# A new order for the same operations: attention and a squared-ReLU network on one core

## The chip, the core and the metric

The kernel runs on one core of one Trainium2 chip. Such a core has five engines that run side by side, each working through its own queue of instructions in order: TensorE (PE, matrix products; its loads of weights are shown apart as PEld), VectorE (DVE), ScalarE (ACT), GpSimd (POOL) and SyncE (SP), which here only issues transfers. Engines wait for each other by semaphores. Transfers between the chip's memory and the core's SBUF run on 16 DMA engines. Products land in PSUM, 8 banks of 2 KB a partition.

The metric is the device time of one execution in microseconds (us). Single executions of this kernel agree within about 0.1%.

## The reference

Inputs are q, k and v of 8 batches, 8 heads, 576 tokens and 64 dimensions, 16 "beacon" tokens of keys and values for each batch and head, and two weight matrices, w_in (512 x 2048) and w_out (2048 x 512).

```python
k_all = np.concatenate([beacon_k, k], axis=2)
v_all = np.concatenate([beacon_v, v], axis=2)
scores = scale * np.matmul(q, k_all.transpose(0, 1, 3, 2))
causal = np.zeros((S, Nb + S), dtype=bool)
causal[:, Nb:] = np.triu(np.ones((S, S), dtype=bool), k=1)
scores = np.where(causal, -1000000000.0, scores)
a = np.exp(scores - scores.max(-1, keepdims=True))
a /= a.sum(-1, keepdims=True) + 1e-09
attn = np.matmul(a, v_all)
x = attn.transpose(0, 2, 1, 3).reshape(B * S, H * D)
h = x @ w_in
r = np.maximum(h, 0.0)
out = (r * r) @ w_out
```

So each of the 4608 tokens gets a causal attention (the beacons are seen by all), and the 512 values of a token then go through a network of 2048 hidden units.

## The kernel before

**The attention.** Work is done a batch and a pair of heads at a time: pair p = 4 x batch + pair, 0 to 31. q and k come from memory in blocks and are transposed, so that the 64 dimensions of a head lie on partitions. Batch 0 and batch 1 are transposed by matmuls: L488 (batch 0, a first part of 240 tokens on the whole array, with 120 rows from two head pairs at a time, and a second part of 336 tokens, tp0.1.*, on halves of the array's columns, 64 at a time), L490 (batch 1, on halves of the columns too), and L453 for the beacons on 32 rows. From batch 2 on DMA transposes do it. The scores (L650, names qk) use halves of the array's rows: the two heads of a pair lie on 64 rows each. ACT takes the exponential (L672 in batch 0, L748 later), POOL (L777) or DVE (L781) masks the diagonal, and the product with v (L803, av) uses the whole array, with a column of ones that gives the sum. DVE takes the reciprocal (L820) and normalizes (L822, norm) out of PSUM into xn. xn is transposed to xT by matmuls (L871, xtp, with a copy xte) or by DMA.

**The network** works on nine chunks of 512 tokens, each as soon as its tokens' attention is there. Chunks 0 to 2 multiply by w_in plainly (L1093, s1), take relu (L1107 on ACT, L1109 on DVE) and the square (L1117, L1119); chunk 0 also multiplies by w_out plainly (L1142, s2). Later ones use seven products of halves in place of eight, with sums of weights (L929, L914) and of activations (L963, L966, L1171, L1174) made by DVE and POOL; their products are L990 and L1206, the partial results are kept in `spare` (L373, L375), joined (L1028) and squared (L1054, L1056), and the outputs are summed by DVE (L1229) and stored.

**Loads.** The first blocks of q and k come through SP and ACT, the other loads are issued by POOL: q (L409), k and v (L418, their beacons L417), strided blocks of q and k of batches 0 and 1 (L473), the four quarters of w_in (L894) and of w_out (L903). v has two buffers, one for even and one for odd batches.

**What sets the order.** Every operation is recorded under a name, and one long string, SEQUENCE (lines 17 to 167), lists all 1737 names. `Order.run` goes through it and issues each operation to its engine; a letter behind @ chooses the engine (A is ACT, D is DVE, P is POOL). Each engine then runs its own instructions in this order. Buffers that are shared (two `strip` tiles of two PSUM banks for the scores, four `ps` banks for all else, three `held` areas) are handed out first come first served, as the string goes.

```python
for word in SEQUENCE.split():
    name, _, letter = word.partition("@")
    op = named.pop(name)
    e = self.LETTER[letter] if letter else op.engs[0]
```

60 dummy matmuls (L355, fill, 128x256 on a tile of ones) are names in the string too; they go to places at the start where the order's maker expected TensorE to be idle.

Of the kernel before, what the change touches and what calls it, by code (L numbers as in the profile page):

```python
# [29 lines left out]
norm1.0.0 exp1.1.0 exp0.1.0 qk1.1.2 av3.0.0 norm0.0.0 tp0.1.3q fill18 fillg18 qk2.0.0 fill47 fillg47 norm3.0.0  # L30
exp1.1.2 exp2.0.0 eq0.1.3@D tpg0.1.3q tp0.1.2k fill45 fillg45 xtp0.0.0 fill0 xtp0.0.1 ek0.1.2@D tpg0.1.2k fillg0
qk0.1.2 mask2.0.0@D xte0.0.1@A xte0.0.0@D win0 qk0.1.1 fill4 fillg4 av2.0.0 fill56 fill24 fillg56 fill14 fill30
fillg24 fillg30 fillg14 norm2.0.0 tp0.1.2q fill5 tp0.1.3k fillg5 xtp0.0.2 xtp0.0.3 eq0.1.2@D exp0.1.2 exp0.1.1 qk1.1.1
xte0.0.2@A qk2.1.0 exp1.1.1 xte0.0.3@D s1.0.5.0 s1.0.6.0 mask0.1.1@P ld1v2 win3 bkc1 ek0.1.3@D exp2.1.0 mask0.1.0@P
sld1k0.0 mask1.1.1@P ld1v1 ld2q4 ld2q0 zero2 sld1q0.0 sld1k0.2 wout0 sld1q0.2 wout1 ld1v0 ld2k0 wout2 ld2q5 ld1v4
wout3 ld1v3 ld2k2 ld2q1 ld2q7 ld2k3 tpg0.1.2q tpg0.1.3k qk2.1.1 exp2.1.1 s1.0.4.0 s1.0.9.0 qk2.1.2 qk3.1.0 mask2.1.1@D
relu0.4.0@D relu0.9.0@D s1.0.10.0 mask2.1.0@D mask1.1.0@D relu0.6.0@A relu0.10.0@A exp3.1.0 av0.1.0 norm0.1.0 s1.0.7.0
av1.1.0 exp2.1.2 relu0.5.0@A s1.0.11.0 relu0.7.0@D sq0.3.0@A relu0.11.0@D norm1.1.0 mask3.1.1@D qk3.1.1 qk3.1.2
s1.0.2.0 s1.0.1.0 exp3.1.1 mask3.1.0@D relu0.1.0@D xtp0.1.1 exp3.1.2 xte0.1.1@A relu0.2.0@A av2.1.0 s1.0.0.0 xtp0.1.0
av3.1.0 norm2.1.0 relu0.0.0@D xte0.1.0@A s1.0.3.0 relu0.3.0@A norm3.1.0 s1.0.14.0 xtp0.1.2 s1.0.13.0 xtp0.1.3  # L40
relu0.14.0@A xte0.1.2@A s1.0.12.0 s1.0.8.0 relu0.13.0@D relu0.12.0@D relu0.8.0@D xte0.1.3@A s1.0.6.1 relu0.6.1@A
s1.0.13.1 s1.0.2.1 tpb1 ekb1 relu0.2.1@D s1.0.0.1 relu0.0.1@A relu0.13.1@D s1.0.11.1 relu0.11.1@A s1.0.1.1 s1.0.15.0
relu0.15.0@A sq0.7.0@A relu0.1.1@D tp1.0.0q s1.0.10.1 relu0.10.1@D tp1.0.0k ek1.0.0 eq1.0.0@A tpg1.0.0q tp1.0.1q
tp1.0.1k eq1.0.1@D s1.0.12.1 qk4.2 sq0.1.0@D relu0.12.1@A ek1.0.1 tpg1.0.1q tpg1.0.0k tpg1.0.1k s1.0.4.1 s1.0.7.1
relu0.7.1@D sq0.2.0@D s1.0.5.1 s1.0.14.1 relu0.4.1@A exp4.2.0.0.0 mask4.0.0.0@D relu0.5.1@A sq0.0.0@D exp4.2.1.0.0
s1.0.15.1 s1.0.9.1 relu0.9.1@D s1.0.3.1 qk4.4 sq0.3.1@D relu0.3.1@A relu0.15.1@D sq0.0.1@A sq0.1.1@D exp4.4.1.0.0
s1.0.8.1 tp1.0.2k tp1.0.2q relu0.8.1@D relu0.14.1@D sq0.4.0@A sq0.2.1@D sq0.6.1@D sq0.5.0@D sq0.4.1@D exp4.4.0.0.0
mask4.0.2@P ek1.0.2 s2.0.2.0 s2.0.0.0 s2.0.2.1 eq1.0.2@A sq0.5.1@D tpg1.0.2q tpg1.0.2k qk5.7 exp5.7.-1.1.0
exp5.7.1.0.0 exp5.7.-1.0.0 s2.0.0.1 tp1.0.3k exp5.7.0.0.0 mask4.0.0.1@P ld2q3 mask6.0.0.0@P ld2k4 ld2q2 ld2q6
mask4.0.1.1@D wsum1 mask4.0.1.0@D s2.0.0.2 tp1.0.3q s2.0.2.2 sq0.7.1@D ek1.0.3 eq1.0.3@A asum1 mask5.0.2@D  # L50
mask5.0.1.1@D tpg1.0.3k sq0.6.0@A tpg1.0.3q qk7.13 exp7.13.-1.0.0 s2.0.2.3 ev0.2@D exp7.13.0.0.0 exp7.13.-1.1.0
exp7.13.1.0.0 s2.0.0.3 s2.0.3.0 ev0.0@A mask5.0.0.1@P mask7.0.0.1@D mask7.0.1.0@D mask7.0.1.1@D mask7.0.2@D ld2v0
mask5.0.1.0@P ld2k1 ld2v2 qk6.10 exp6.10.-1.1.0 exp6.10.1.0.0 exp6.10.0.0.0 exp6.10.-1.0.0 mask6.0.1.1@P mask6.0.0.1@P
s2.0.3.1 av4.0.0 s2.0.3.2 mask7.0.0.0@D mask5.0.0.0@D av5.0.0 mask6.0.2@P mask6.0.1.0@D norm5.0.0 av7.0.0 norm7.0.0
norm4.0.0 tr2q tr2k s2.0.3.3 av6.0.0 av4.0.1 ev0.3@A s2.0.1.0 norm4.0.1 norm6.0.0 av6.0.1 av7.0.1 norm6.0.1 av5.0.1
s2.0.1.1 norm7.0.1 norm5.0.1 xtp1.0.0 xtp1.0.2 xte1.0.2@D xte1.0.0@A s2.0.1.2 xtp1.0.3 xtp1.0.1 s2.0.1.3 xte1.0.1@A
xte1.0.3@D s1.1.13.0 relu1.13.0@A asum2 s1.1.4.0 wsum2 relu1.4.0@D s1.1.15.0 ev0.1@A relu1.15.0@A s1.1.6.0 relu1.6.0@D
qk8.2 exp8.2.1.0.0 exp8.2.0.0.0 s1.1.7.0 s1.1.2.0 s1.1.0.0 qk8.4 relu1.7.0@A relu1.2.0@A exp8.4.1.0.0 s1.1.1.0
s1.1.14.0 relu1.1.0@A relu1.14.0@A exp8.4.0.0.0 s1.1.5.0 relu1.0.0@D mask8.0.0.0@D wsum3 wsum4 relu1.5.0@D s1.1.11.0
s1.1.12.0 sq1.2.0@A warm sq1.0.0@D relu1.11.0@D sq1.3.0@D s1.1.3.0 relu1.12.0@A sq1.6.0@A mask8.0.1.0@D s1.1.10.0  # L60
s1.1.8.0 s1.1.9.0 relu1.10.0@A relu1.3.0@D qk9.7 relu1.9.0@A exp9.7.-1.0.0 mask8.0.2@D mask8.0.0.1@D sq1.7.0@D
sq1.1.0@D mask8.0.1.1@D sum1.1.1@D sq1.5.0@D ld3q4 ld2v3 ld3q2 ld2v1 ld3q5 ld2v4 ld3v2 ld3q1 ld3k4 ld3k3 ld3k0 ld3q0
ld3v3 ld3k2 ld3q6 ld3q7 ld3k1 st1 st0 av8.0.0 relu1.8.0@D sq1.4.0@A exp9.7.-1.1.0 s2.1.1.0 av8.0.1 norm8.0.0
sum1.3.1@D s2.1.1.1 sum1.1.0@D sum1.3.0@D sum1.2.1@D sum1.2.0@D s2.1.2.0 s2.1.5.0 s2.1.2.1 exp9.7.1.0.0 exp9.7.0.0.0
ev1.c1.None@A norm8.0.1 ev1.c11.None mask9.0.0.1@D ld3v0 ld3q3 ld3v4 mask9.0.1.0@P mask9.0.1.1@P mask9.0.0.0@D tr3k
s2.1.6.0 qk10.10 s2.1.6.1 exp10.10.-1.0.0 exp10.10.-1.1.0 exp10.10.0.0.0 exp10.10.1.0.0 xtp2.0.0 mask9.0.2@D av9.0.0
s2.1.5.1 xte2.0.0@A mask10.0.1.0@P sum1.4.1@D ev1.u2.None@D s2.1.7.0 av9.0.1 s2.1.7.1 ev1.u3.None@A norm9.0.0
norm9.0.1 mask10.0.2@P mask10.0.0.1@P ld4k4 sum1.4.0@D mask10.0.0.0@D tr3q ld4k0 ld4q7 ld4q6 ld4k2 mask11.0.0.0@D
mask10.0.1.1@D qk11.13 exp11.13.-1.0.0 exp11.13.-1.1.0 exp11.13.1.0.0 exp11.13.0.0.0 s2.1.4.0 av10.0.0 s2.1.4.1
xtp2.0.1 mask11.0.1.0@P mask11.0.1.1@P mask11.0.0.1@P ev1.c22.None norm10.0.0 mask11.0.2@D ev1.c21.None@D xte2.0.1@A  # L70
s2.1.3.0 av10.0.1 norm10.0.1 qk12.2 exp12.2.0.0.0 av11.0.0 xtp2.0.2 av11.0.1 norm11.0.0 xte2.0.2@A exp12.2.1.0.0
s2.1.3.1 norm11.0.1 xtp2.0.3 xte2.0.3@A ev1.c12.None qk12.5 exp12.5.-1.0.0 exp12.5.1.0.0 s1.2.3.0 relu2.3.0@D
exp12.5.-1.1.0 exp12.5.0.0.0 s1.2.2.0 s1.2.9.0 s1.2.10.0 relu2.2.0@D asum4 qk13.8 relu2.9.0@A exp13.8.-1.0.0
exp13.8.1.0.0 exp13.8.-1.1.0 s1.2.6.0 s1.2.8.0 s1.2.0.0 exp13.8.0.0.0 mask12.0.1.0@D relu2.10.0@D relu2.6.0@D s1.2.1.0
# [1280 lines left out]
```

## Time and profile before

| | |
|---|---|
| median of 3 runs | 322.87 us (322.85 to 323.05) |
| the profiled execution | 323.34 us |
| its span, first to last instruction | 321.6 us |
| mean granted clock of TensorE | 0.998 |
| DMA traffic | 39.61 MB, mean 123 GB/s |

The page of the profile gives for each engine its busy time, its share of the span and its number of instructions. The timeline lists runs of instructions of the same kind on one engine: start and length in us, engine, line, operation, what it writes and reads, how many; a bracket at the end says how long the engine had been idle before and what released it. The length of such a run ends with the modelled end of its last matmul, which overlaps the next run, so two runs are compared from start to start. The chain of waits follows the end of the program back to its start, and its rows are start, length, engine, tile and line. The windows give the busy time of every engine in a stretch of the span (from:to, length, then each engine in the order of the head line, the granted clock, the mean number of busy DMA engines' share as listed, and GB/s).

The work falls into these stretches: to 7.84 us, first loads and dummy matmuls; to 19.72, batch 0's transposes, scores and av up to the first product with w_in; to 42.88, the rest of batch 0, chunk 0 against w_in and the first transposes of batch 1; to 68.92, chunk 0 against w_out, the other transposes and the first attention of batch 1; to 256, the attention of the other batches between the chunks; to 318, the last chunks alone; then the last sum and store.

### The profile page before, as it was taken

How to read it: one execution, taken by the hardware profiler on the slowest of the kernel's cores; microseconds unless marked ns; L12 is line 12 of the kernel's file. 1: busy time of each engine (PE TensorE's matmuls, PEld its weight loads, DVE VectorE, ACT ScalarE, POOL GpSimd, SP SyncE). 2: the span in 40 equal slices, each digit the busy share in tenths (PEclk: the TensorE clock that was granted, in tenths of full speed). 3: DMA queues.
4: the chain of work that ended last, by engine and by line, in shares of the span. 5: the costliest groups of instructions: out<-in, count | busy, mean ns of one | idle time of the engine just before them, and what ended most of it. 6: DMA issues, size and time to landing. Idle time of an engine off the chain costs nothing.

```text
span 321.6 us, 9484 instructions
## 1 busy us (share of the span) xinstructions
PE 314.5 (98%) x3882; PEld 247.3 (77%) x3882; DVE 249.6 (78%) x526; ACT 217.1 (68%) x324; POOL 196.9 (61%) x316
## 2 busy tenths in 40 slices
PE   7999999999999999999999999999999999999995
PEld 5679755744887469889888878888888878888884
DVE  2977696759966699879987999798877987697852
ACT  2787589268678694679678896889696653763320
POOL 9675387398169737697794779625436060555651
PEclk9999999999999999999999999999999999999999
DMA  8999999999969999999989959993701230110042
GB/s 154 184 193 191 197 182 124 222 162 130 175 53 119 138 177 154 127 171 193 105 123 178 190 56 126 142 126 95 128 2 67 79 65 0 67 65 2 16 151 98
DMA packets 153189, 39.61 MB, mean 123 GB/s; under 512 B 140730, under 2 KB 148794, under 8 KB 153146
## 3 DMA queue, kind: packets, MB, share of 16 engines
q0 software_dynamic: 103744, 18.10, 72.8%
q1 hardware_dynamic: 48253, 20.29, 30.0%
q10 hardware_dynamic: 1149, 0.62, 0.9%
q8 instruction: 30, 0.49, 0.6%
q14 instruction: 13, 0.11, 0.1%
HBM read 37.22 MB, written 9.44 MB: 145 GB/s over the span
## 4 chain that ended last, share of the span: by engine, by line
PE 91%; DVE 5%; issue 1%; ACT 1%; DMA 1%; POOL 0%; DVEq 0%; ACTq 0%; POOLq 0%
PE ps L1206 28%; PE ps L990 21%; PE ps L1093 13%; PE ps L803 8%; PE strip L650 7%; PE ps L1142 4%; PE ps L355 3%; PE ps L650 2%; PE strip L1206 2%; DVE g L1028 2%; DVE xn L822 1%; PE ps L871 1%; PE ps L488 1%; PE ps L490 1%; DMA xT<-xn 1%
## 5 line engine op out<-in xcount | busy, mean ns | idle before, releaser
L1206 PEld LDWEIGHTS <-g 128*128 128x128 bf16 x768 | 72.7, 97 | 10.6 <-issue 1.2
L748 ACT ACTIVATE pt<-strip 128x1024 bf16<-128x1024 f32 x70 | 70.9, 1032 | 5.4 <-PE strip L650 5.4
L1206 PE MATMUL ps<-w_out,g 128*128 128x256 bf16 x480 | 61.0, 272 | 0.0
L1028 DVE CUSTOM_DVE_ANT_0 g<-ps,spare 128x512 bf16<-128x512 f32 x72 | 48.7, 686 | 15.7 <-PE ps L990 11.2
L777 POOL TENSOR_SCALAR_AFFINE_SELECT pt<-pt 128x256 bf16<-128x256 bf16 (+1 forms) x78 | 31.9, 429 | 45.1 <-ACT pt L748 41.6
L373 ACT COPY spare<-ps 128x512 f32<-128x512 f32 x54 | 31.6, 588 | 23.9 <-PE ps L990 17.0
L1093 PE MATMUL ps<-xT,w_in 128*128 128x512 bf16 (+2 forms) x256 | 45.2, 326 | 0.0
L990 PEld LDWEIGHTS <-w_in 128*128 128x128 bf16 x480 | 39.4, 96 | 7.0 <-issue 2.5
L409 POOL DMA_DIRECT2D qk_area<-in_q_dram x48 | 35.0, 733 | 13.2 <-DMA qT<-qk_area 6.8
L990 PE MATMUL ps<-xT,w_in 128*128 128x256 bf16 (+4 forms) x384 | 41.8, 247 | 0.7 <-DVE g L1056 0.7
L1174 POOL TENSOR_TENSOR g<-g 128x256 bf16<-128x256 bf16 x44 | 29.6, 708 | 18.4 <-DVE g L1171 12.6
L803 PE MATMUL ps<-vb,pt 128*128 128x65 bf16 (+1 forms) x960 | 38.2, 193 | 0.1
L803 PEld LDWEIGHTS <-pt 128*128 128x128 bf16 (+1 forms) x960 | 35.5, 97 | 3.3 <-issue 0.6
L1093 PEld LDWEIGHTS <-w_in 128*128 128x128 bf16 x256 | 23.6, 98 | 17.2 <-issue 2.0
L418 POOL DMA_DIRECT2D vb<-in_v_dram x40 | 34.0, 851 | 1.2 <-DMA qk_area<-in_q_dram 0.7
L822 DVE TENSOR_TENSOR xn<-ps,rcp 128x320 bf16<-128x320 f32 (+2 forms) x64 | 31.5, 492 | 2.2
L1054 ACT ACTIVATE g<-g 128x1024 bf16<-128x1024 bf16 x30 | 31.1, 1067 | 2.3 <-DVE g L1028 1.5
L990 PEld LDWEIGHTS <-qk_area 128*128 128x128 bf16 x320 | 27.5, 97 | 5.5 <-issue 1.7
L748 ACT ACTIVATE pt<-ps 128x512 bf16<-128x512 f32 x42 | 24.0, 601 | 8.1 <-PE ps L650 6.9
L1206 PE MATMUL ps<-w_sum,g 128*128 128x256 bf16 x224 | 28.9, 272 | 0.0
L650 PEld LDWEIGHTS <-kT 64*128 64x128 bf16 x618 | 20.0, 94 | 11.1 <-issue 8.8
L418 POOL DMA_DIRECT2D qk_area<-in_k_dram x30 | 25.4, 850 | 4.2 <-DMA kT<-qk_area 1.8
(87 smaller groups left out, 502.0 us busy)
## 6 DMA issues: line engine op xcount, KB each, us to landing
out_dram<-osb SPq DMA_DIRECT2D x16, 512.0 KB, 3.5
qk_area<-in_q_dram POOLq DMA_DIRECT2D x48, 72.0 KB, 4.9
vb<-in_v_dram POOLq DMA_DIRECT2D x24, 128.0 KB, 6.0
qk_area<-in_k_dram POOLq DMA_DIRECT2D x18, 128.0 KB, 4.5
w_in<-in_moe_w_in_dram POOLq DMA_DIRECT2D x4, 512.0 KB, 10.9
w_out<-in_moe_w_out_dram POOLq DMA_DIRECT2D x4, 512.0 KB, 10.6
vb<-in_v_dram POOLq DMA_DIRECT2D x8, 112.0 KB, 4.4
qk_area<-in_k_dram POOLq DMA_DIRECT2D x6, 112.0 KB, 4.7
```

The costliest lines, as they stand in the source:

```text
L373: nc.scalar.copy(dst, src)
L409: return [nc.gpsimd.dma_start(out=qb[:, g, :, D * u:D * u + D], in_=t[b, c].rearrange("(n p) d -> p n d", p=NP))]
L418: insts.append(nc.gpsimd.dma_start(out=dst[lo:rows], in_=t[b, :, t0:t0 + rows - lo, :].transpose([1, 0, 2])))
L650: nc.tensor.matmul(out, kc[b % 2][hp, c, pr] if b >= NPE else kT[b % 2][hp, pr, 128 * c:128 * c + 128], rhs, start=True, stop=True)
L748: nc.scalar.activation(out, in_, AF.Exp, bias=0.0, scale=scale)
L777: nc.gpsimd.affine_select(out=d[:, :, i], in_=d[:, :, i], compare_op=ALU.is_ge, fill=0.0, base=Nb if m0 + i == 0 else 0, pattern=[[0, 2], ...
L803: nc.tensor.matmul(a[:, at + (t - tl[0]) * (D + 1):at + (t - tl[0] + 1) * (D + 1)], P[0:rr, hj, o:o + 128], vb[b % 2][0:rr, c, 2 * pr + hj ...
L822: nc.vector.tensor_tensor(out=xn[b % 2].rearrange("p t (h d) -> p h t d", d=D)[:, h0:h0 + nh, tl[0]:tl[0] + nt], in0=a[:, :, :, 0:D], in1= ...
L990: nc.tensor.matmul(o[:, i * HT + at:i * HT + at + w], lhs[:, m, f * 128:(f + 1) * 128], part[:, m], start=fresh and i == 0 and at == 0 and ...
L1028: nc.vector._custom_dve(TENSOR_ADD_SAT, out=dst, in0=bank_of(chain), in1=held[keep[added].held[1]].rearrange("p (f t) -> p f t", f=2), s0= ...
L1093: nc.tensor.matmul(h[:, lo - spans[0][0]:hi - spans[0][0]], w_in_sb[:, mc, ft * 128:(ft + 1) * 128], xT[:, mc, lo % RING:lo % RING + hi - lo],
L1206: nc.tensor.matmul(o, lhs[:, f, t * 128:(t + 1) * 128], rhs[:, f], start=fresh and f == 0, stop=f == HF - 1, skip_group_check=True)
```

## The change

Only the string SEQUENCE differs: a new order of the same 1737 names, and for some of them another engine. All code below it is the same, so the same instructions are issued. The first two lines of each stand for the rest:

```diff
-ones fill23 fillg23 fill54 fill58 fillg58 fillg54 fill12 fill15 fill53 fillg53 fillg15 fill7 fillg7 ident tri fill29
-fillg12 fill57 fill22 fillg22 fill43 fillg43 fillg57 fill33 fillg29 fill16 fill40 fillg40 fillg16 fill13 fillg13 fill6
...
+ones fill25 fillg25 fill59 fill30 fill18 fillg18 fillg59 fill29 fill14 fillg30 fillg14 fill8 fillg8 fillg29 fill50 fillg50
...
```

What it moves shows in the order of instructions on the engines. In the excerpts the rows are line, operation, output<-inputs and size; a matmul stands behind the load of its weights.

**TensorE, just ahead of the first product with w_in.** Here the last column-split transposes of batch 0 (L488 with 64 rows), the transposes of xn (L871, whole array) and scores (L650, row-split) follow each other. Before:

```order
L488 LDWEIGHTS qk_area
L488 MATMUL ps_94<-ident,qk_area 64x112
L871 LDWEIGHTS xn_75
L871 MATMUL ps_95<-ident,xn_75 128x112
L871 LDWEIGHTS xn_75
L871 MATMUL ps_95<-ident,xn_75 128x128
L871 LDWEIGHTS xn_75
L871 MATMUL ps_93<-ident,xn_75 128x112
L871 LDWEIGHTS xn_75
L871 MATMUL ps_93<-ident,xn_75 128x128
L650 LDWEIGHTS kT_69
L650 MATMUL strip_91<-qT_67,kT_69 128x208
```

After:

```order
L488 LDWEIGHTS qk_area
L488 MATMUL ps_92<-ident,qk_area 64x112
L650 LDWEIGHTS kT_69
L650 MATMUL strip_91<-qT_67,kT_69 128x208
L650 LDWEIGHTS kT_69
L650 MATMUL strip_91<-qT_67,kT_69 128x208
```

The transposes of xn have moved ahead of the column-split ones, and these now touch the scores.

**TensorE, among the products of chunk 0 with w_out.** The transposes of batch 1 (L490, column-split) stand between L1142 (whole array). Before, one of the places where they are parted:

```order
L490 LDWEIGHTS qk_area
L490 MATMUL ps_92<-ident,qk_area 64x96
L1142 LDWEIGHTS g_80
L1142 MATMUL ps_95<-w_out,g_80 128x512
L1142 LDWEIGHTS g_80
L1142 MATMUL ps_95<-w_out,g_80 128x512
L1142 LDWEIGHTS g_80
L1142 MATMUL ps_95<-w_out,g_80 128x512
L1142 LDWEIGHTS g_80
L1142 MATMUL ps_95<-w_out,g_80 128x512
L490 LDWEIGHTS qk_area
L490 MATMUL ps_94<-ident,qk_area 64x96
```

After, where the first 12 of a visit end (bank ps_95) and the next 12 begin (ps_92):

```order
L490 LDWEIGHTS qk_area
L490 MATMUL ps_95<-ident,qk_area 64x96
L490 LDWEIGHTS qk_area
L490 MATMUL ps_92<-ident,qk_area 64x96
L490 LDWEIGHTS qk_area
```

Five visits of 12, 36, 24, 12 and 12 transposes have become three of 48, 24 and 24.

**POOL, the loads for batch 5's values** (vb_66; vb_65 is batch 6's, L1174 a sum of four pieces for chunk 3). Before, from the last of the early loads to the sums and on:

```order
L418 DMA qk_area<-in_k_dram 80x8x64
L409 DMA qk_area<-in_q_dram 96x6x64
L1174 TENSOR_TENSOR g_81<-g_81 128x256 x8
L418 DMA qk_area<-in_k_dram 112x8x64
L777 AFFINE_SELECT pt<-pt 128x2x128
L418 DMA vb_66<-in_v_dram 128x8x64
L417 DMA qk_area<-in_beacon_k_dram 16x8x64
```

After:

```order
L1174 TENSOR_TENSOR g_81<-g_81 128x256 x4
L417 DMA vb_66<-in_beacon_v_dram 16x8x64
L418 DMA vb_66<-in_v_dram 112x8x64
L418 DMA qk_area<-in_k_dram 128x8x64
L418 DMA vb_66<-in_v_dram 128x8x64
L418 DMA vb_66<-in_v_dram 80x8x64
L418 DMA qk_area<-in_k_dram 128x8x64 x2
```

Before, one block of batch 5's values stood behind the sums; now there are three, the first, the second and the last.

Other moves that matter to what follows: on POOL the three loads `ld0v2 win1 win2` (a v block of batch 0 and quarters 1 and 2 of w_in) became `win2 win1 ld0v2`; of the 60 dummy matmuls 41 in place of 34 stand ahead of the beacon transposes (L453); the av operations of batch 1's first pairs are spread among L1142 and L871; `warm` (L567, a small exponential on ACT) moved from before batch 2's attention to the attention of pair 22; the sums and copies of the later chunks moved by a place or two, some to another engine.

More of the change, by code (lines that the diff above doesn't have):

```diff
@@ L58 @@
[L58 to L62, printed above, removed]
@@ new lines @@
+ld6v4 mask21.0.1.1@P exp23.13.1.0.0 exp23.13.0.0.0 av21.0.0 norm21.0.0 s1.4.1.4 s1.4.1.3 s1.4.2.7 h4.1.c21@D h4.1.c12
+av20.0.1 s1.4.3.1 norm20.0.1 h4.2.u3@A s1.4.2.5 s1.4.2.4 h4.3.c1@A h4.2.c21@A s1.4.3.6 av21.0.1 h4.2.c22 sq4.1.1@D
+tr6k xt4.4 st7 st6 xt4.3 norm21.0.1 s1.4.2.3 h4.2.c12 h4.3.u2@A s1.4.3.7 h4.3.u3@D sq4.2.0@D qk22.11 sq4.1.0@A warm
+exp22.11.-1.0.0 exp22.11.0.0.0 exp22.11.-1.1.0 s1.4.3.5 s1.4.3.2 s1.4.3.4 h4.3.c22 s1.4.3.3 mask22.0.1.0@D h4.3.c11
+h4.3.c12 mask22.0.0.0@P mask23.0.1.1@P mask23.0.2@P mask22.0.0.1@P ld7q5 ld7q6 ld7q4 ld7q3 ld7q0 mask23.0.1.0@P
```

288 lines of the change are left out of this document (145 added, 143 removed).

## The prediction

> **What bounds the kernel now.** I read the page first: busy shares, then the chain of work that ended last.
>
> ```profile
> PE 314.5 (98%) x3882; PEld 247.3 (77%) x3882; DVE 249.6 (78%) x526; ACT 217.1 (68%) x324; POOL 196.9 (61%) x316
> PE 91%; DVE 5%; issue 1%; ACT 1%; DMA 1%; POOL 0%; DVEq 0%; ACTq 0%; POOLq 0%
> ```
>
> TensorE (PE) is busy 314.5 of 321.6 us and holds 91% of the chain. No matmul is added or removed, so the change can only act on three things: how PE moves from one matmul to the next, the 9% of the chain on other engines, and waits that do not exist yet. The busy time by stretches says where these can lie.
>
> ```profile
> core 0: us, PE busy (x) PEld busy (x) DVE busy (x) ACT busy (x) POOL busy (x), PEclk, DMA share, GB/s
> 7.84:19.72 11.88, 11.88 (x175) 7.65 (x175) 10.04 (x31) 9.15 (x16) 7.85 (x12) 1.00 1.68 186
> 42.88:68.92 26.04, 25.90 (x304) 14.54 (x300) 19.63 (x44) 16.06 (x25) 18.11 (x28) 1.00 1.62 164
> 256.00:318.00 62.00, 61.53 (x544) 52.59 (x544) 45.60 (x73) 27.45 (x44) 29.62 (x44) 1.00 0.19 61
> ```
>
> From 7.84 us on PE looks full, but the first of these rows (batch 0, up to the first w_in product) is filled by dummy matmuls (L355): 26 of the 60 lie in it. There PE can also be waiting for others and not show it. DVE (10.04 of 11.88) and ACT (9.15) are dense too, and DMA moves 186 GB/s. The granted clock is 1.00, so that no clock effect is to be had. The rest is a PE-bound pass.
>
> A busy PE still hides one cost. I read it from the timeline of PE, start to start:
>
> ```profile
> 35.62 1.12 PE L490 MATMUL ps<-ident,qk_area 96*64 96x96 bf16 x36
> 36.66 0.64 PE L1093 MATMUL ps<-xT,w_in 128*128 128x272 bf16 x4
> ...
> 42.24 0.70 PE L490 MATMUL ps<-ident,qk_area 96*64 96x96 bf16 x24
> 42.88 1.47 PE L1142 MATMUL ps<-w_out,g 128*128 128x512 bf16 x6
> ...
> 47.33 0.45 PE L490 MATMUL ps<-ident,qk_area 96*64 96x96 bf16 x12
> 47.71 1.04 PE L1142 MATMUL ps<-w_out,g 128*128 128x512 bf16 x4
> 48.68 0.45 PE L490 MATMUL ps<-ident,qk_area 96*64 96x96 bf16 x12
> ...
> 56.47 1.08 PE L803 MATMUL ps<-vb,pt 128*128 128x65 bf16 x30
> 57.38 1.03 PE L1142 MATMUL ps<-w_out,g 128*128 128x512 bf16 x4
> 58.25 1.12 PE L803 MATMUL ps<-vb,pt 128*128 128x65 bf16 x30
> 59.51 1.02 PE L1142 MATMUL ps<-w_out,g 128*128 128x512 bf16 x4
> ```
>
> Four L1142 matmuls between whole-array neighbours take 58.25 - 57.38 = 0.87 us; the same four ahead of column-split transposes (L490) take 48.68 - 47.71 = 0.97. So going into another split of the array costs 0.10 us. Two visits of 12 transposes take 2 x 0.38 = 0.76, one visit of 24 takes 42.88 - 42.24 = 0.64: coming back costs 0.12. The visit of 36 takes 1.04 against 3 x 0.38 = 1.14, by which a return costs 0.05; but something else waits in it, since 24 further transposes at (0.64 - 0.38)/12 = 0.022 us each would make 0.38 + 0.52 = 0.90, so 0.14 of it is a wait. I take 0.10 us a change, between 0.05 and 0.12.
>
> **The change part by part.** *Changes of split.* I counted them in the order of TensorE of both programs: 117 before, 108 after. Row-split are the scores (L650), column-split the transposes L490 and those of L488 with 64 rows, on 32 rows L453, everything else is on the whole array. Of the nine saved, five lie ahead of the first w_in product: two row-split visits became one (twice one change), and three times a column-split visit now touches a row-split one directly instead of through a fill or an xn transpose. The other four are the L490 visits, five before and three after (12, 36, 24, 12, 12 transposes become 48, 24, 24). From about 69 us on both programs change equally often. Nine at 0.10 are 0.9 us, from 0.45 to 1.1.
>
> The Trainium skill, "TensorEngine Tiling (Array Packing)", Key Properties, says that changing the tiling mode drains the TensorE. It gives no time there; "TensorE: Matmul & The Clock Gate", Single matmul latency, puts the drain at about 175 ns. By that, an estimate, nine changes would be 1.6 us in place of 0.9. The rows here give a bit over half of it, and I stay with them.
>
> *First stage: -0.27.* Its five changes are 0.50 us only if PE sets its end. ACT may:
>
> ```profile
> 10.85 1.46 ACT L672 ACTIVATE pt<-strip 128x736 bf16<-128x736 f32 x2
> 12.20 0.45 ACT L373 CAST qT<-ps 128x336 bf16<-128x336 f32 x1
> 12.61 3.13 ACT L672 ACTIVATE pt<-strip 128x736 bf16<-128x736 f32 x4
> 15.94 0.78 ACT L672 ACTIVATE pt<-strip 128x736 bf16<-128x736 f32 x1 [0.20 <-PE strip L650]
> 19.25 0.53 PE L650 MATMUL strip<-qT,kT 64*128 64x208 bf16 x10
> 19.72 0.99 PE L1093 MATMUL ps<-xT,w_in 128*128 128x240 bf16 x8
> ```
>
> From 10.85 to 16.7 the exponentials run nearly without a gap, and av, norm, xn transpose and the product at 19.72 hang on them. The fills stay 60, only 41 instead of 34 stand ahead of the beacon transposes, which start later by the same PE work that is then missing behind them; the first exponential should start within 0.2 us of 10.85. Between 0 and -0.5, I take the middle, rounded up a little: the last four changes lie behind the dense piece of ACT.
>
> *w_in quarter: +0.1.* On POOL's queue a v block of batch 0 and then w_in quarters 1 and 2 were issued; now quarter 2, quarter 1, then that block. The product at 19.72 reads quarter 1.
>
> ```profile
> 7.70 0.90 POOL L418 DMA_DIRECT2D vb<-in_v_dram  x1
> 9.01 1.62 POOL L894 DMA_DIRECT2D w_in<-in_moe_w_in_dram  x2 [0.41 <-DMA qk_area<-in_k_dram]
> w_in<-in_moe_w_in_dram POOLq DMA_DIRECT2D x1, 512.0 KB, 10.4
> ```
>
> The last row is the second of the two, issued at about 9.8: it landed at 20.2. Quarter 1 is now this second one, with a 128 KB block less ahead of it, 0.7 us at the 186 GB/s above: 19.5, where PE asks at 19.45. At worst, without that relief, it is 0.75 late. Behind its wait PE's whole queue stands, so it would count in full. The block of v that falls back (128 KB, 0.7 us of traffic) is first read by the av matmuls at about 22.5 and has cover.
>
> *Batch 1: -0.4.* PE has no fills there, the row 42.88:68.92 shows 25.90 of 26.04 busy, and all four changes are on the path. *The wait at 59.5: -0.3.* Thirty av matmuls take 0.91 at 56.47 but 1.26 at 58.25. Their end is held by a norm, the step that frees the accumulator:
>
> ```profile
> 58.96 0.50 DVE xn L822
> 59.47 0.04 issue
> 59.51 1.02 PE ps L1142 x4
> ```
>
> Three norms of 0.7 us stood in a row on DVE while av ran 75 matmuls in 2.9 us. The new order spreads av among L1142 and the transposes of xn, which need no accumulator from a norm; that gives 0.35 back, unless DVE's sums of weights (about 1.2 us each), which now stand nearer, delay a norm: then it is +0.3. I take -0.3. *The 0.14 in the visit of 36*: the merged visit of 48 takes the same four banks; -0.1, or 0.
>
> *From 69 us: +0.15.* The order is new here too, without a change of split saved. The waits that PE shows are few, and their causes stay:
>
> ```profile
> PE ps L990 <- DVE g L1056: 0.7, 1, 0.7
> PE ps L990 <- DVE g L1028: 0.4, 1, 0.4
> L373 ACT COPY spare<-ps 128x512 f32<-128x512 f32 x54 | 31.6, 588 | 23.9 <-PE ps L990 17.0
> ```
>
> At 185.9 the hold chain on DVE before a block of 60 av, at 256 the last chunk's transposes and sums: the same operations follow one another there, and I give 0. At four or five places one ACT copy (0.59 us) or mask now stands ahead of an exponential or behind a sum; each shows up as a fraction of 0.59, about 0.1, together some 0.4. The old order has such places too, and I let half of theirs go: +0.15, between -0.3 and +0.6. ACT's warm-up operation moves to where ACT idles: 0. The tail behind the last w_out product is in the same order: 0.
>
> *Sum*: -0.27 + 0.1 - 0.4 - 0.3 - 0.1 + 0.15 = -0.82 on the profiled execution of 323.34 (span 321.6, 1.74 around it): 322.52. The median of the runs shown, 322.87, lies 0.47 below that execution, so 322.05. With the bounds it goes from -0.5 - 0.4 - 0.35 - 0.14 - 0.3 = -1.7 to +0.75 + 0.3 - 0.2 + 0.6 = +1.45 (four changes at 0.05): 321.2 to 324.3.
>
> **The rivals.** *No difference.* The first stage is set by ACT and the w_in quarter, and what batch 1 gains is given back in the 250 us behind it, where PE merely meets later a transfer or a norm that has not become earlier. For it: the chain of the first stage, and waits at 185.9 and 256 that end with DVE. Against it: PE is 98% busy between, and DMA lands well ahead. 0 + 0.1 - 0.4 + 0.3 = 0, with the wait at 59.5 merely moved: 322.9.
>
> *Slower: the v blocks of batch 5.* POOL now does one more sum of four pieces (L1174) ahead of three v blocks that the attention of head pair 20 needs; before, two of them were issued over 15 us earlier.
>
> ```profile
> 160.37 3.32 POOL L1174 TENSOR_TENSOR g<-g 128x256 bf16<-128x256 bf16 x4 [2.22 <-DVE g L1171]
> 163.64 0.93 POOL L418 DMA_DIRECT2D qk_area<-in_k_dram  x1
> vb<-in_v_dram POOLq DMA_DIRECT2D x1, 80.0 KB, 7.2
> DMA to landing us min/median/max: 3.2/5.2/10.5
> 173.86 0.46 PE ps L803 x15
> ```
>
> The sum must wait for the same DVE sums as the one in the row, so it ends at about 163.6; four issues of 0.9 later, near 167.3, stands the last v block. At the median of 5.2 it lands at 172.5, at 7.2 at 174.5, at the slowest 10.5 at 177.8. The av matmuls ask at about 173.9. So it decides from a landing of 6.6 us on; near 9.7 us, as a late one of these loads shows under transposes, PE stands 3.1 us with scores behind it: -0.82 + 3.1 = +2.3, 325.1; at 8.5 us it stands 1.9, which gives 323.9. I put 324.5. Against it: between 160 and 176 the transposes of batch 6 begin only behind these loads.
>
> *Slower, smaller: w_in.* Quarter 1 lands as the second did, 20.2, and the quarter read next moves too: +0.75 and as much again for DVE's weight sums: 322.05 - 0.1 + 1.5 = 323.45.
>
> *Faster by more.* All nine at 0.12 with the first stage bound by PE, and nothing lost later: -1.5: 321.4.
>
> **How the numbers follow.** The chances: forecast 0.46, faster by more 0.10, no difference 0.22, the v blocks 0.11, w_in 0.11. The likeliest, 322.05, has a range of its own of 321.5 to 322.6. The overall range starts at the fast rival's time and reaches up over the w_in case to the middle of the v blocks' (323.9): 321.3 to 323.9. One measurement of this kernel tells 0.2%, 0.65 us, from no change, which puts the border at 322.22, inside the forecast's own range: of its 0.46 I count 0.35 as faster and 0.11 as the same. With the other cases: faster 0.45, same 0.33, slower 0.22.
>
> **What would show it.** *Right*: the first L1093 starts at 19.3 to 19.6; L490 shows three visits, of about 1.2, 0.64 and 0.64 us; no gap like 58.25 to 59.51; the time won up to 69 us is 0.8 to 1.1. *Wrong*: the first L1093 waits for w_in or starts at 19.7; a visit of 48 takes longer than 1.2; PE stands ahead of L803 at 174 with a DMA as releaser; or the win at 69 us is there and the last w_out product starts no earlier, which would make the later order the cause.

## The result, and the profile after

The changed kernel takes 324.59 us (median of 14 runs, 323.0 to 325.13); the kernel before, run beside it, 323.1 (14 runs, 322.75 to 324.54). The ratio is 1.0034, 95% interval 1.0018 to 1.0049: slower by 0.34%, where 322.05 was forecast. Its executions also lie 2.1 us apart, those of the kernel before, but for one, within 1.2: the 0.1% that its first three runs suggested was too narrow.

The first profiled execution is the fastest of the 14, 323.0 us with a span of 321.3. Its page, busy shares and the chain that ended last:

```profile
PE 312.5 (97%) x3872; PEld 246.1 (77%) x3882; DVE 248.6 (77%) x527; ACT 216.9 (68%) x327; POOL 191.7 (60%) x306
PE 90%; DVE 7%; issue 1%; ACT 1%; DVEq 0%; ACTq 0%
```

Ten matmul records are missing in this trace (x3872), so most of the 2 us by which PE is busy for less is no gain. DVE holds 7% of the chain in place of 5: the chain that ends last runs over it for longer. A second profile, of an execution of 325.7 us (span 324.0), shows what PE waited for; the columns are the sum in us, how often, the longest:

```profile
PE ps L355 <- DVE ones L349: 1.8, 1, 1.8
PE ps L803 <- POOL pt L777: 1.2, 1, 1.2
PE ps L990 <- ACT spare L373: 0.7, 1, 0.7
PE ps L990 <- DVE g L1028: 0.6, 2, 0.3
PE ps L990 <- DVE spare L963: 0.5, 1, 0.5
PE ps L1206 <- DVE g L1171: 0.4, 1, 0.4
```

The first row, the start, is the same in all. The second, av behind a mask on POOL, is not there in the first profile nor before. The last is in both profiles of the new order and not before.

Where the time went shows when two traces are matched matmul by matmul. The table gives, at places where PE has done the same set of work in all, how much later (+) or earlier (-) than before it begins the next operation, in us; "us before" is the time in the trace of before.

| us before | what follows there | first profile | second profile | new head, old rest | old head, new rest |
|---|---|---|---|---|---|
| 7.84 | beacon transposes | 0.00 | +1.11 | +0.78 | -0.38 |
| 19.72 | first L1093 | -0.86 | +0.23 | -0.09 | -0.38 |
| 64.51 | end of batch 1's stage | -1.72 | -0.40 | -0.84 | -0.38 |
| 122.2 | ahead of pair 15's av | -1.78 | -0.46 | -0.83 | -0.43 |
| 127.3 | behind its first block | -1.76 | +0.99 | -0.83 | +0.54 |
| 161.8 | chunk 3 against w_out | -1.62 | +1.13 | -0.90 | +0.89 |
| 209.4 | chunk 5 | -1.34 | +1.41 | -0.90 | +0.80 |
| 253.0 | ahead of the last chunks | -1.17 | +1.59 | -0.90 | +0.98 |
| 285.6 | chunk 8 | -0.42 | +2.30 | -0.91 | +1.40 |
| 316.9 | last product | -0.32 | +2.41 | -0.91 | +1.50 |

The last two columns are experiments told of below. The gain is made by 64.5 us, and from there on the new order loses 1.4 us in the first profile, 2.8 in the second and 1.9 in the one with the old head.

The stage of batch 1 did what the diff says. PE's timeline of the first profile, start to start, shows three visits of column-split transposes:

```profile
31.72 1.21 PE L490 MATMUL ps<-ident,qk_area 96*64 96x96 bf16 x48
32.92 0.62 PE L1093 MATMUL ps<-xT,w_in 128*128 128x272 bf16 x4
...
41.95 0.70 PE L490 MATMUL ps<-ident,qk_area 96*64 96x96 bf16 x24
42.58 1.04 PE L1142 MATMUL ps<-w_out,g 128*128 128x512 bf16 x4
...
57.32 0.62 PE L803 MATMUL ps<-vb,pt 128*128 128x65 bf16 x15
57.78 0.42 PE L871 MATMUL ps<-ident,xn 112*128 112x112 bf16 x5
58.04 1.08 PE L803 MATMUL ps<-vb,pt 128*128 128x65 bf16 x30
58.95 1.03 PE L1142 MATMUL ps<-w_out,g 128*128 128x512 bf16 x3
```

48 transposes take 1.20, 24 take 0.63, and thirty av matmuls 0.91 in place of 1.26: the wait at 59.5 is gone.

### The profile page after: what moved, and what is told of

Read it like the earlier page. It is cut to its first block, busy times and chain, and to the rows that moved or that the text cites. A ratio compares the mean times of both kernels' runs of the same rounds, so it can differ in the third digit from the quotient of the medians.

```text
span 321.3 us, 9452 instructions
## 1 busy us (share of the span) xinstructions
PE 312.5 (97%) x3872; PEld 246.1 (77%) x3882; DVE 248.6 (77%) x527; ACT 216.9 (68%) x327; POOL 191.7 (60%) x306
## 4 chain that ended last, share of the span: by engine, by line
PE 90%; DVE 7%; issue 1%; ACT 1%; DVEq 0%; ACTq 0%
PE ps L1206 26%; PE ps L990 22%; PE ps L1093 13%; PE ps L803 8%; PE strip L650 7%; PE ps L1142 4%; PE ps L355 3%; PE ps L650 2%; PE strip L1206 2%; DVE g L1028 2%; PE ps L871 1%; PE ps L488 1%; DVE xn L822 1%; DVE spare L963 1%; PE ps L490 1%
## 5 line engine op out<-in xcount | busy, mean ns | idle before, releaser
L1028 DVE CUSTOM_DVE_ANT_0 g<-ps,spare 128x512 bf16<-128x512 f32 x72 | 48.9, 686 | 15.9 <-PE ps L990 13.3
L777 POOL TENSOR_SCALAR_AFFINE_SELECT pt<-pt 128x256 bf16<-128x256 bf16 (+1 forms) x76 | 29.5, 410 | 47.0 <-ACT pt L748 45.1
L373 ACT COPY spare<-ps 128x512 f32<-128x512 f32 x57 | 33.3, 590 | 24.8 <-PE ps L990 16.5
L1093 PE MATMUL ps<-xT,w_in 128*128 128x512 bf16 (+2 forms) x251 | 44.0, 325 | 0.3 <-issue 0.2
L803 PE MATMUL ps<-vb,pt 128*128 128x65 bf16 (+1 forms) x960 | 37.1, 193 | 0.0
L803 PEld LDWEIGHTS <-pt 128*128 128x128 bf16 (+1 forms) x960 | 34.6, 97 | 3.1 <-issue 0.4
L1093 PEld LDWEIGHTS <-w_in 128*128 128x128 bf16 x256 | 23.8, 98 | 16.9 <-issue 1.7
L1174 POOL TENSOR_TENSOR s_sum<-g 128x256 bf16<-128x256 bf16 x24 | 16.1, 698 | 30.7 <-ACT g L1054 19.9
L1174 POOL TENSOR_TENSOR g<-g 128x256 bf16<-128x256 bf16 x36 | 24.6, 710 | 13.0 <-ACT osb L373 6.6
L1054 ACT ACTIVATE g<-g 128x1024 bf16<-128x1024 bf16 x28 | 28.7, 1060 | 0.8 <-DVE g L1028 0.7
L990 PE MATMUL ps<-spare,qk_area 128*128 128x256 bf16 x192 | 28.0, 272 | 0.6 <-DVE spare L963 0.6
```

The lines of the kernel that those rows point to most:

```text
L373: nc.scalar.copy(dst, src)
L777: nc.gpsimd.affine_select(out=d[:, :, i], in_=d[:, :, i], compare_op=ALU.is_ge, fill=0.0, base=Nb if m0 + i == 0 else 0, pattern=[[0, 2], ...
L803: nc.tensor.matmul(a[:, at + (t - tl[0]) * (D + 1):at + (t - tl[0] + 1) * (D + 1)], P[0:rr, hj, o:o + 128], vb[b % 2][0:rr, c, 2 * pr + hj ...
L990: nc.tensor.matmul(o[:, i * HT + at:i * HT + at + w], lhs[:, m, f * 128:(f + 1) * 128], part[:, m], start=fresh and i == 0 and at == 0 and ...
L1028: nc.vector._custom_dve(TENSOR_ADD_SAT, out=dst, in0=bank_of(chain), in1=held[keep[added].held[1]].rearrange("p (f t) -> p f t", f=2), s0= ...
L1093: nc.tensor.matmul(h[:, lo - spans[0][0]:hi - spans[0][0]], w_in_sb[:, mc, ft * 128:(ft + 1) * 128], xT[:, mc, lo % RING:lo % RING + hi - lo],
```

## The experiments

All times are medians; each ratio is against the kernel before, run on the same chip beside it.

**The changed kernel again.** No edit.

> The changed kernel once more, for a profile of one of its usual executions (median 324.59 against 323.0 for the one profiled first, which is its fastest of 14). Theory A (the early gain is there in every execution, and the loss lies in the later order): the first L1093 starts at 18.6 to 19.0, the stretch to 65 us is 1.4 to 1.9 us shorter than before, and some 1.5 us of waits that the fast execution does not show stand behind 69 us, on PE ahead of an av or L990 matmul. Theory B (what varies is the first stage: loads of w_in or of batch 0 that land late): the first L1093 starts at 19.5 or later, and the later waits are those of the fast execution.

324.33 us, 323.11 to 326.09, ratio 1.0037 (1.0016 to 1.0057). Both theories had half of it. The later waits are theory A's; the first L1093 at 19.95 is theory B's, so the head varies too, but not by its loads, as the start shows. PE's timeline from the start, in the first profile and then in the second:

```profile
1.81 6.10 PE L355 MATMUL ps<-ones 128*128 128x256 bf16 x41 [1.81 <-DVE ones L349]
7.84 0.25 PE L453 MATMUL ps<-ident,w_sum 16*128 16x16 bf16 x4
18.86 0.99 PE L1093 MATMUL ps<-xT,w_in 128*128 128x240 bf16 x8
```

```profile
1.81 7.21 PE L355 MATMUL ps<-ones 128*128 128x256 bf16 x41 [1.81 <-DVE ones L349]
8.95 0.25 PE L453 MATMUL ps<-ident,w_sum 16*128 16x16 bf16 x4
19.95 0.99 PE L1093 MATMUL ps<-xT,w_in 128*128 128x240 bf16 x8
```

The same 41 dummies took 6.10 and 7.21 us. In both traces they first follow each other at 0.21 us and then at 0.109; the step falls after 14 of them (4.77 us) in the one and after 25 (7.11 us) in the other. Everything up to the first L1093 moves with it, by 1.1 us. The head of before moves too: with the step at 5.6 us (the run with the old head, below) its first L1093 began at 19.34, with the step at 6.4 at 19.72. The prediction read "no clock effect" from a granted clock of 1.00 behind 7.84 us; this effect comes from the stretch ahead of that.

**The two halves of the order.** Old and new order cut at the same work, about 65 us: first the new head with the old rest, then the old head with the new rest. In the first, as an order of names:

```diff
 SEQUENCE = new order up to xte1.0.3,
-           the rest of the new order
+           what is left, in the order of before
```

> The new order up to the last output copy of batch 1's transposes (about 65 us), then the order of before for all that is left. Theory A: the head keeps its gain of 1.4 to 1.9 us, the old rest loses none of it or half of it: 321.2 to 322.2, below the kernel before in every round. Theory B: as slow as the changed kernel, 324 or more, with its spread of 2 us. A third theory, that the early gain is worth nothing because a transfer or chain behind it does not move: 322.7 to 323.1.

322.67 us (321.56 to 323.09), ratio 0.9979 (0.9966 to 0.9993).

> The mirror of it: the order of before up to the same point (about 65 us), then the new order. Theory A: it has the loss and not the gain: 324.59 + 1.7 = 326.0 to 326.5. Theory B: the loss is gone, 322.7 to 323.3. Third theory (the early gain is worth nothing): as the changed kernel, 324.6.

325.24 us (323.83 to 326.36), ratio 1.0065 (1.0044 to 1.0085). So the head gains 0.4 us by medians and the rest loses 2.2. Their sum, 1.8, is a little above the 1.3 that the whole loses on that chip. Both effects came out smaller than theory A's numbers (321.2 to 322.2 and 326.0 to 326.5), which took the head's 1.7 us from the first profile. By its time alone, 322.67 would as well be the third theory's (322.7 to 323.1); the trace decides against it. The profiled execution with the new head had its step at 6.46 us, as the one of before (6.44): at equal steps the head gained 0.09 us to the first L1093, 0.84 to 64.5, and nothing of it was lost in the old rest. The medians show less, 0.4: of this pair of executions, the one of before (323.34) is 0.3 above the median of before beside this run (323.04), and the new one (322.41) 0.3 below its own.

**The old order for the last two chunks.** New order to 254 us, then the old one.

> The new order up to about 254 us, then the order of before for the last two chunks. In the fast execution the early gain of 1.8 us was down to 1.2 at 254 us and to 0.3 at the end. If the last chunks' order is what loses: 323.6 to 323.8 (about 0.9 below the changed kernel). If the loss lies between 69 and 254 us: 324.4 to 324.8, as the changed kernel.

323.4 us, ratio 1.0002 (0.9990 to 1.0014), 0.9 below the changed kernel on the same chip and a little below what was expected. By its trace the tail is 0.4 of that (it lost 0.44 us behind 253 where the second profile above lost 0.82). Its profiled execution had no wait at pair 15; how often its others had one is not known.

**What happens at pair 15.** The order of POOL there, with the semaphores that an instruction waits for, names eight for POOL's transfers in rotation (DMASW0 to 7; a part is left out):

```
L418 DMA vb_65<-in_v_dram 128x8x64 [waits DMASW3_49,PE_49]
...
L409 DMA qk_area<-in_q_dram 96x6x64 [waits DMASW2_49]
L409 DMA qk_area<-in_q_dram 96x6x64 [waits DMASW3_49]
L417 DMA qk_area<-in_beacon_k_dram 16x8x64 [waits DMAHW0_49,DMASW4_49]
L418 DMA qk_area<-in_k_dram 112x8x64 [waits DMASW5_49]
L418 DMA qk_area<-in_k_dram 128x8x64 [waits DMASW6_49]
L418 DMA qk_area<-in_k_dram 80x8x64 [waits DMASW7_49]
L418 DMA qk_area<-in_k_dram 128x8x64 [waits DMASW0_49]
L409 DMA qk_area<-in_q_dram 96x6x64 [waits DMASW1_49]
L777 AFFINE_SELECT pt<-pt 128x2x128 [waits DVE_49,Activation_49]
```

Each transfer waits for the semaphore that it will itself raise, so it is issued only when the eighth before it has landed, whatever that one loads, and POOL's masks (L777) stand behind it. The second profile, POOL's timeline and then PE's:

```profile
116.94 0.73 POOL L409 DMA_DIRECT2D qk_area<-in_q_dram  x1
119.92 0.73 POOL L409 DMA_DIRECT2D qk_area<-in_q_dram  x1 [2.25 <-DMA vb<-in_v_dram]
120.64 0.54 POOL L417 DMA_DIRECT2D qk_area<-in_beacon_k_dram  x1
121.16 3.32 POOL L418 DMA_DIRECT2D qk_area<-in_k_dram  x4
124.47 0.73 POOL L409 DMA_DIRECT2D qk_area<-in_q_dram  x1
125.21 0.77 POOL L777 TENSOR_SCALAR_AFFINE_SELECT pt<-pt 128x256 bf16<-128x256 bf16 x2
```

```profile
123.74 1.05 PE L1206 MATMUL ps<-w_sum,g 128*128 128x256 bf16 x8
126.04 1.09 PE L803 MATMUL ps<-vb,pt 128*128 128x65 bf16 x30 [1.25 <-POOL pt L777]
```

POOL stood 2.25 us for the landing of a v block, then issued seven transfers in 5.3 us, and only then masked. In the first profile the stop was 0.85 us and the masks were done at 123.2, when PE asked at 123.3. I call this theory M and tried three ways to take the wait away.

> The changed kernel with one edit: on POOL the two masks of pair 15 stand ahead of six loads of batch 5 (q block 6, k blocks 0, 3, 4, 2, q block 3) instead of behind them. Theory M (POOL issues a load only when the eighth load before it has landed, so the masks, and with them the av of pair 15, wait for landings, 0 to 1.4 us by the execution): no wait ahead of the av of pair 15 in the profile, median 0.6 to 1.0 below the changed kernel's 324.3 to 324.6, so 323.4 to 323.9, and less spread. Rival (the loads that now come later move the wait to the next user of POOL or to batch 5's transposes): 324.3 or more, with a wait of like size behind 130 us.

```diff
-ld5q6 ld5k0 ld5k3 ld5k4 ld5k2 ld5q3
 ...
 mask15.0.0.1@P mask15.0.0.0@P
+ld5q6 ld5k0 ld5k3 ld5k4 ld5k2 ld5q3
 qk16.2 ld4v4
```

328.49 us, ratio 1.0158 (1.0138 to 1.0178): the rival. The wait at pair 15 is gone, but the last v block of batch 4 is issued behind the moved loads, at 129.7. The chain of waits of this run:

```profile
129.66 7.00 DMA vb<-in_v_dram
136.66 0.04 issue
136.70 0.19 PE ps L803
```

The av of pair 16 stood 3.2 us from 133.1 on. A mask of that pair was late too, since it stood behind the same loads on POOL; PE's timeline puts 2.72 us of the wait down to it, and the v block came last:

```profile
132.05 1.04 PE L1206 MATMUL ps<-w_sum,g 128*128 128x256 bf16 x8
132.93 0.44 PE L803 MATMUL ps<-vb,pt 128*128 128x65 bf16 x9
136.08 0.81 PE L803 MATMUL ps<-vb,pt 128*128 128x65 bf16 x6 [2.72 <-POOL pt L777]
136.73 1.62 PE L1206 MATMUL ps<-w_sum,g 128*128 128x256 bf16 x8
138.29 0.62 PE L650 MATMUL ps<-qT,kT 64*128 64x16 bf16 x6
```

The wait is not the whole loss. Eight products took 0.88 us ahead of it and 1.56 behind it, and this window gives the reason:

```profile
137.03:140.44 3.41, 3.41 (x31) 2.02 (x30) 3.38 (x7) 1.49 (x3) 1.31 (x3) 0.50 0.68 64
```

From 137.03 to 140.44 us the granted clock was 0.50. Matched with before, PE lost another 1.4 us in it.

> The changed kernel with both suspects undone: the masks of pair 15 ahead of the six loads, and the old order for the last two chunks. If losses add: the old tail alone gave 323.4, less what the masks still cost there on average (0.5 to 0.9): 322.5 to 322.9. What is then left against the new head with the old rest (322.67) is the waits at 160 us (0.5) and 205 us (0.45), less 0.2 to 0.3 won at 184 to 188 us.

328.07 us, ratio 1.0152 (1.0137 to 1.0167), with a wait at the same place (2.9 us, this time ended by the mask) and 3.41 us at a granted clock of 0.50 behind it. It says nothing on the sum.

> The changed kernel with one edit that moves no load: the two masks of pair 15 that stood on POOL behind six loads run on DVE, at the same place of the order. Theory M (these two masks behind POOL's loads are the wait that differs from execution to execution): no wait ahead of the av of pair 15, no new one at the av of pairs 16 to 18; median 323.4 to 323.9 in place of 324.3 to 324.6, lowest and highest closer together than 2 us. Rival (DVE is late there too, or the wait moves on as in the last try): 324.3 or more.

```diff
-mask15.0.0.1@P mask15.0.0.0@P
+mask15.0.0.1@D mask15.0.0.0@D
```

328.26 us, ratio 1.0158 (1.0143 to 1.0173): the rival again, in the other form that it names. Its DVE timeline, and then what PE waited for:

```profile
122.81 0.49 DVE L781 TENSOR_TENSOR pt<-pt,tri 128x256 bf16<-128x256 bf16 x2 [2.95 <-ACT pt L748]
123.22 0.69 DVE L1171 TENSOR_TENSOR g<-g 128x1024 bf16<-128x1024 bf16 x1
```

```profile
PE ps L1206 <- DVE g L1171: 3.4, 2, 3.0
```

The masks need exponentials that ACT ends at 122.8. In front of the sums (L1171) they made DVE idle for 2.95 us and the product that reads these sums late by 3.0; here too the granted clock was 0.50 for the next 3.41 us.

> The changed kernel with the two masks of pair 15 on DVE, but behind the four sums that the next w_out product needs, where the last try had them ahead; no load is moved. Theory M (behind POOL's loads these two masks are the wait that differs between executions, 0 to 1.4 us): no wait over 0.4 us at the av of pair 15 nor at the product before it; median 323.3 to 323.9 against 324.3 to 324.6. Rival (any other place costs as much): 324.3 or more.

```diff
-mask15.0.0.1@P mask15.0.0.0@P
 ...
 sum2.3.0@D sum2.2.0@D
+mask15.0.0.1@D mask15.0.0.0@D
 s2.2.6.0 norm13.0.1 av15.0.0
```

323.01 us (322.58 to 324.09), ratio 1.0001 (0.9989 to 1.0012). Two masks, moved from behind POOL's loads to behind DVE's sums, take the loss against before away: theory M, and 0.3 below its range. In this trace PE goes from the product (122.45) to the av (123.33) without a wait. It is the fastest of the twelve executions, though, and the first profile had no wait there either, so the times are the evidence and not the trace. A wait at 205 us, told of below, is not there either, which may be the 0.3. The rest is still worse than the old one: by this trace it loses 1.1 of the 1.8 us that the head had gained at 93 us.

> The same with the old order for the last two chunks. If the two losses add: 323.4 (old tail alone) less 0.5 to 0.9: 322.5 to 322.9, so below the kernel before. If not: 323.2 or more.

323.05 us, ratio 0.9989 (0.9977 to 1.0002). Against the run without the old tail no gain can be told by the times; by the traces the stretch behind 253 us lost 0.5 without it and 0.2 with it. That the two losses add is left open.

**One part of the change alone.** The kernel before, with the five visits of batch 1's transposes joined to three and nothing else moved:

```diff
-tp1.0.0q s1.0.10.1 relu0.10.1@D tp1.0.0k
+s1.0.10.1 tp1.0.0q relu0.10.1@D tp1.0.0k
...
-s2.0.0.1 tp1.0.3k ... s2.0.0.2 tp1.0.3q
+s2.0.0.1 s2.0.0.2 tp1.0.3k ... tp1.0.3q
```

> The kernel before with two operations moved on PE, so that its five visits of column-split transposes of batch 1 become three (48, 24, 24), as in the change; nothing else is moved. Theory S (a change of the array's split costs 0.10 us of PE, four are saved): PE is 0.35 to 0.45 us earlier from 50 us on and keeps that to the end: ratio 0.9986 to 0.9989. Rival (the gain of the head came from other moves, a change of split costs nothing by itself or is swallowed): the same time as before from 50 us on.

322.41 us, ratio 0.9977 (0.9967 to 0.9987). This is theory S with more than it expected. In the trace PE is level with before at 33.7 us (+0.04), 0.28 earlier at 37.8 and 0.51 earlier from 50.8 to 153 us. There a further 0.2 is won, where the chain of before runs over DVE (L1028, which ends at 153.53); it is 0.74 at the end. The first join gave 0.32 (two changes and the 0.14 of waiting that the prediction put into the old visit of 36), the second 0.23. So a change of split costs 0.09 to 0.12 us, the lower value if that 0.14 is right.

**The dummies.** Seven of the 41 dummies ahead of the beacon transposes moved behind the last product, with the new head and the old rest:

> The new head with the old rest (measured 322.67), with the last 7 of the 41 dummy matmuls ahead of the beacon transposes moved behind the last product of the program, where PE is idle; 34 are left ahead, as before the change. Theory C (the dummies run at 0.21 us each until the array's clock comes up, at a time between 4.8 and 7.1 us that differs from execution to execution, and at 0.107 behind it, so that 41 of them and not a load set the start of the transposes): the beacon transposes start 0.75 us earlier for the same time of full clock, the first L1093 0.4 to 0.75 earlier, the end likewise: 321.9 to 322.3. Rival (the casts of the first blocks, so the loads, set that start): the beacon transposes wait, nothing is won, 322.6 to 322.8.

322.16 us, ratio 0.9968 (0.9957 to 0.9979), theory C. By the ratios this is 0.4 us better than with 41, and the two intervals overlap; the traces tell more. The step fell late, at 7.33 us, as in the run with the masks ahead of the loads; there 41 dummies let the beacon transposes begin at 9.06 and L1093 at 20.32, here 34 at 8.31 and 19.37. The 0.75 of the first difference is the seven dummies at 0.109 each; the 0.2 that the second has on top is a wait for DVE in the other execution.

> As the run with 34 dummies ahead of the beacon transposes (322.16), with 7 more of them moved to the end, 27 left ahead. If the dummies still set the start: another 0.3 to 0.75 less, 321.5 to 321.9. If now the casts of the first blocks set it (ACT's last one ended at 8.2 there, the transposes of q and k began at 8.6): 0 to 0.4 less, 321.8 to 322.2, with a wait of PE ahead of its first L488 and a start of L1093 that no longer depends on the time of full clock.

321.27 us, ratio 0.9948 (0.9935 to 0.9960). PE now waits 0.9 us for a cast inside the first transposes, as the second form says, but the time is below both forms; no run says why.

> As the run with 34 dummies ahead (322.16), with the 19 dummies between the beacon transposes and the first L1093 moved to the end. If they only fill waits for ACT and DVE: the same first L1093 within 0.1 us and 322.0 to 322.3. If they delay PE: the first L1093 up to 1 us earlier and 321.2 to 321.9. If the array's clock needs them: matmuls at half speed behind 8 us and 322.5 or more.

321.56 us, ratio 0.9953 (0.9941 to 0.9966), first L1093 at 18.36: the 19 dummies between did delay PE, and the clock does not need them. The step fell early in this execution (4.76 us) and a cast held the transposes up to 8.40. From there to L1093 it is 9.96 us; in the run with the 19 dummies it was 10.75, from its first transposes at 8.62.

> The new head with the old rest, 27 dummies ahead of the beacon transposes, none between them and the first L1093, the other 33 at the end of the program: both edits that won by themselves (321.27 and 321.56). If they add (less PE work in the first stage, and its start no longer set by the dummies): 320.7 to 321.2. If ACT's exponentials already set the end of the first stage: 321.2 to 321.6. If the clock falls back for want of work: matmuls at half speed behind 8 us, 322 or more.

322.48 us, ratio 0.9979 (0.9969 to 0.9990), worse than either, though L1093 began at 17.87. PE's timeline shows why:

```profile
314.55 1.04 PE L1206 MATMUL ps<-w_out,g 128*128 128x256 bf16 x8
315.42 0.49 PE L355 MATMUL ps<-ones 128*128 128x256 bf16 x3
316.10 3.44 PE L355 MATMUL ps<-ones 128*128 128x256 bf16 x30 [0.19 <-DVE osb L1229]
```

33 dummies behind the last product end at 319.5 and set the end. Without them, NFILL set to what is left:

> The last kernel without its 33 dummies at the end (27 in all, all ahead of the beacon transposes). The profile of the last one showed PE 2.4 us ahead of the kernel before at 308 us, and the 33 dummies running to 319.5 us, behind the last useful product at 315.6, so that they set the end. If so: 322.48 less 1.0 to 1.4 us, 321.1 to 321.5, or lower if its profiled execution is typical: 322.87 - 2.4 = 320.5. If the clock or ACT was the reason: 322.3 to 322.6 again.

321.22 us, ratio 0.9946 (0.9933 to 0.9959).

> As that, with 34 dummies ahead of the beacon transposes. If the dummies there only cost: 0.2 to 0.6 above the kernel with 27. If they bring the clock up earlier or bridge the wait for the first casts: the same or below it.

321.01 us (320.56 to 321.89), ratio 0.9936 (0.9922 to 0.9950): no worse than with 27, the two are not told apart. It is the run of 321.56 without its 26 dummies at the end. It beats both kernels: the new head, the old rest, and 34 dummies in place of 60.

## Why the prediction was wrong

**The failed step is "From 69 us: +0.15".** It took the causes of PE's few waits to "stay", and priced the new order of the 250 us behind by some places with "a fraction of 0.59" each. By medians that order cost 2.2 us with the old head. The traces show 0.9 to 1.4 us lost there in the three executions of the table, and up to 1.4 more that differs. The steady part is chains, above all on DVE, that now end later than PE. Two of them in the chain of waits of the first profile:

```profile
158.52 0.69 DVE g L1171
159.22 0.05 issue
159.26 1.92 PE ps L1206 x16
...
204.46 0.70 DVE g L1028
205.16 0.04 issue
205.20 2.84 PE ps L990 x24
```

The same places before, where the chain stays on PE:

```profile
156.12 0.49 PE ps L803 x15
156.62 6.19 PE ps L1206 x56
...
206.22 0.46 PE ps L803 x15
206.68 2.70 PE ps L990 x24
```

That is 0.5 us at 159 and, in some of the traces, 0.45 at 205, then 0.2 at 220 and 0.5 to 0.8 in steps of 0.2 to 0.3 in the last chunks; some 0.5 won between 130 and 185 us goes off it. Which of the moved operations makes each chain late was not tried. The quoted waits of before said that DVE and ACT are close behind PE there, and the prediction read them as fixed instead of as a sign that another order of the same operations can lose as much at each.

**The part that differs is a rival with its place wrong.** "The v blocks of batch 5" saw loads on POOL's queue come too late for an av. At pair 20 they did not: the sum ended at 161.9, the last block was issued at 165.0 and landed at 169.0, 4 us ahead of the av. But the mechanism was there 50 us earlier, with masks instead of a v block behind the loads, and the trial with the loads moved gave it in the very form of the rival, at pair 16. That it came to 3.2 us where 3.1 had been worked out is chance: the 3.1 was for a landing of 9.7 us, the block here landed in 7.0. The prediction asked when a load lands; it did not ask what compute stands behind the loads on POOL and what a stop of the queue does to it.

**Changes of split: right.** 0.10 us was taken, 0.09 to 0.12 measured, and the four of batch 1 gave 0.41 without the wait that went with them. The Trainium skill ("TensorEngine Tiling (Array Packing)", Key Properties) says that a change of mode drains the array; the traces show that a change costs time, and not that it is a drain. The 175 ns that the Trainium skill gives for a drain ("TensorE: Matmul & The Clock Gate", Single matmul latency) are more than the runs show.

**Batch 1, the wait at 59.5, and the wait in the visit of 36: right as a sum.** It was -0.8; from the first product to 64.5 us the new head gained 0.75 at equal steps, and no gap like the one at 59.5 is left. The joined visits alone gave 0.55 of it; the rest was not tried alone.

**First stage: right in sign at equal steps, wrong in what sets it.** -0.27 was forecast and -0.09 measured. "PE work that is then missing behind them" took the seven dummies for neutral; but they stand ahead of everything, and cost 0.75 us there. With them PE is what sets the start, in part at half rate, so that the stage depends on when the rate steps up (first L1093 from 18.86 to 20.32 in the profiles with 41). The w_in quarter, +0.1, cost nothing: in the first profile quarter 1 landed at 18.46, ahead of its product at 18.86.

Up to 64.5 us the forecast was -0.97, with -0.84 in the traces at equal steps and -0.4 by medians. Without the +0.15 for the rest, 321.90 would have stood against the 322.67 measured with the old rest: the head's forecast was nearer to one pair of traces than to the times.

## What to carry to other kernels

Price a new order by its whole length, not by the part that it was made for: on an engine that is 98% busy, every chain that ends just behind it is worth a few tenths of a microsecond at each place, and here they, with the wait at pair 15, outweighed nine saved changes of split. On a queue that both loads and computes, look for compute behind a burst of loads; its delay varies from execution to execution, so one profile may miss it. A wait of about 3 us costs more than itself, since the matmuls behind it ran at half rate for 3.41 us. Dummy work ahead of the first real work is paid in full as soon as it lasts longer than the loads and casts that the real work waits for.

## What the runs showed of the hardware

The dummies, of 256 columns, follow each other at 0.21 us and then at 0.109; the step came between 4.5 and 7.5 us in the 18 profiles, 2.7 to 5.7 us after the first dummy at 1.81. The granted clock of the windows stands at 1.00 ahead of it too, but the traces hold no record of the clock there: the first one lies at the step (at 4.82 us in the first profile, at 7.08 in the second). The Trainium skill ("TensorE: Matmul & The Clock Gate", What's actually happening) puts the step at about 3.4 us of activity, with a window that does not start with the kernel; half rate and a varying step agree, the spread seen here is wider than the 0.5 us either way given there.

The rate falls again behind a long wait. Behind waits of 2.7, 2.7 and 3.0 us (the two runs with the masks ahead of the loads, and the one with them on DVE ahead of the sums) the granted clock was 0.50 for 3.41 us, 1.00 before and after. In the other 15 profiles no wait behind the first dummy was above 1.25 us, and none shows a fall ahead of the last product. Where between 1.25 and 2.7 us the border lies, no run shows.

Without such a wait the clock stays up without dummies: with 34 or 27 at the start and no others ahead of the first L1093, waits of up to 1.0 us behind them and of 0.2 later, eight score matmuls took 0.90 to 0.93 us, as in the other traces.
